# Linear attention with an ELU feature map: v loaded in longer rows, z from one-column products on held weights, five tiles added by GpSimd, one exp for the transposed q

## The chip, the cores and the metric

The kernel runs on one core of a Trainium2 chip. The metric is the device time in microseconds of one execution. The core has five engines that run side by side and meet by semaphores: TensorE (PE in the profile; its weight loads are PEld), VectorE (DVE), ScalarE (ACT), GpSimd (POOL) and SyncE (SP), which here only issues DMA transfers. Sixteen DMA engines serve one queue.

## What is computed

```python
phi_q = jnp.where(q > 0, q + 1, jnp.exp(q)) + 1e-6
phi_k = jnp.where(k > 0, k + 1, jnp.exp(k)) + 1e-6
kv  = jnp.einsum("bhsd,bhse->bhde", phi_k, v)
z   = jnp.einsum("bhsd->bhd", phi_k)
num = jnp.einsum("bhqd,bhde->bhqe", phi_q, kv)
den = jnp.einsum("bhqd,bhd->bhq", phi_q, z)[..., None] + 1e-6
return num / den
```

There are 32 heads of 2048 rows by 128 columns in bf16. q, k and v are 512 KB a head each, and so is the result.

## The kernel before

**A head.** A head is 16 tiles of 128 x 128. The feature map is computed as min(exp(x), 1) + 1e-6 plus max(x, 0); these two parts are kept apart as two arrays (emk and rk for k, emq and rq for q), and their sum is formed by PE, which multiplies both parts and accumulates.

- k: ACT takes exp of all 2048 columns (L263), DVE the min and the added 1e-6 (L269), POOL the relu (L265). For four of the 16 tiles (`ADD`, L164) POOL also adds the two parts (L274), so that PE needs one product for such a tile and not two.
- kv and z (L278 to L293): PE accumulates phi_k^T v in one PSUM bank, `kvz_ps`. The column sum z comes by a column of ones beside v. v lies in SBUF in four groups of four tiles with gaps of ones between them (L166, L223), so the first and the last tile of each group take a neighbouring one as a 129th column. A tile inside a group has none beside it, and a second product of one column with the same weights follows (L288). It loads its weights anew. ACT copies kv to SBUF (L294), DVE adds the two parts of z (L296).
- q: PE transposes 16 tiles to `xT_ps` in two halves (L304, two banks). ACT takes exp of each half (L315) and the relu of the second (L318), DVE the relu of the first (L321) and the min (L324).
- result: PE multiplies each q tile's two parts by kv and z (L333, L334), 129 columns a tile, three tiles to each of five PSUM banks, the 16th tile cut over the first two banks. DVE adds 1e-6 to the denominators (L352), takes reciprocals (L356) and multiplies (L364, L369). For the last two heads this is done in two groups of banks, with one bank on ACT (L378).

**Order.** The order on each engine is written by hand: every operation has a key, mostly the head's number plus a constant, and each engine runs its operations by rising key (`Plan.order`). `place` (L239) holds exceptions for the first and last heads. Waits follow from what each operation reads and writes; a PSUM bank read by two engines is read by one after the other.

**Transfers.** SP issues all loads and stores by the same keys (L255, L394). k, v and q have six buffers each, the result ten. k and q go 128 rows of 4096 bytes a head; v goes 512 rows of 1024 bytes, because of its gaps. Stores are put later and later (key h + 1 + 0.18 h, L398), so that at first nearly only loads are issued and at the end only stores are left.

**Ahead of the first head** POOL makes the identity and the ones (L216 to L223), and PE runs 36 products on the identity (L230).

Of the kernel before, what the change touches and what calls it, by code (L numbers as in the profile page):

```python
# [5 lines left out]
ALU = mybir.AluOpType  # L6
# [138 lines left out]
def bass_standalone__linear_attn_elu__prompt_kernel(  # L145
# [15 lines left out]
    NB = 5  # L161
    HALF = NT * P // 2

    ADD = (1, 2, 5, 6)  # L164
    SPLIT = tuple(j for j in range(NT) if j not in ADD)
    GAP, GRP = 32, 4 * D  # L166
    VW = 4 * GRP + 5 * GAP
# [6 lines left out]
    with ExitStack() as es:  # L174
# [39 lines left out]
        ofull = o_ps[:, :]  # L214

        pl.add("pool", -9, lambda g: g.memset(ident[:], 0.0), writes=[("id0",)])  # L216
# [3 lines left out]
        pl.add("pool", -7, lambda g: g.memset(ones_sb[:], 1.0), writes=[("ones",)])  # L220

        vfull = v_sb[:, :, :]
        pl.add("pool", -7, lambda g: g.memset(_ap(vfull, 0, [[VW, NBI], [GAP + GRP, 5], [1, GAP]]), 1.0), writes=[("vones",)])  # L223

        def warm(n):

            def f(pe):
                for w in range(n):
                    b = 2 + w % 3
                    last = pe.matmul(o_ps[:, b * 512 + 3 * NC: b * 512 + 3 * NC + 125], lhsT=ident[:, :], rhs=ident[:, 0:125],  # L230
                                     start=True, stop=True)
                return last
            return f

        pl.add("pe", -9, warm(36), reads=[("ident",)], writes=[("banko", 2), ("banko", 3), ("banko", 4)])

        place = {("emk", 0): -2.05, ("rq", 0): -2.0, ("emq", 0): -1.9, ("zs", 0): -1.75,  # L239
                 ("emk", 1): -1.8, ("rq", 1): -1.7, ("emq", 1): -1.6, ("emk", 2): -1.4, ("rq", 2): 0.945,  # L240
                 ("ek", 1): -0.97, ("ek", 2): 0.03,
                 ("kv", NH - 1): NH - 2 + 0.75, ("kvs", NH - 1): NH - 2 + 0.05, ("zs", NH - 1): NH - 2 + 0.942}

        for h in range(NH):
# [5 lines left out]
            def load(name, buf, src, key, h=h, bi=bi):  # L250
                dst, rws = buf[:, bi], rows(src, h)
                if name == "v":
                    dst = _ap(vfull, bi * VW + GAP, [[GAP + GRP, 4], [1, GRP]])
                    rws = rws.rearrange("p (a b) -> p a b", b=GRP)
                pl.add("sp", key, lambda sp: sp.dma_start(dst, rws), writes=[(name, bi)], dma=(name, bi))  # L255
# [4 lines left out]

# [11 lines left out]
            def added(x, b3=b3):  # L272
                return _ap(x[:, b3, D:2 * D], 0, [[4 * D, 2], [1, 2 * D]])
# [4 lines left out]
            def kv(pe, tiles, srcs, bi=bi, b3=b3):  # L278
                for j in tiles:
                    for src in srcs:  # L280
                        first, fin = (j == SPLIT[0] and src is emk_sb), j == ADD[-1]
                        w = src[:, b3, j * D:(j + 1) * D]
                        c = GAP + (GAP + GRP) * (j // 4) + D * (j % 4)
                        l, r = (1, 0) if j % 4 == 0 else (0, 1) if j % 4 == 3 else (0, 0)
                        last = pe.matmul(kvz_ps[:, 1 - l:NC + r], lhsT=w, rhs=v_sb[:, bi, c - l:c + D + r], start=first, stop=fin,  # L285
                                         skip_group_check=True)
                        if not l + r:
                            last = pe.matmul(kvz_ps[:, 0:1], lhsT=w, rhs=ones_sb[:, 0:1], start=False, stop=fin,  # L288
                                             skip_group_check=True)
                return last  # L290
            pl.add("pe", at("kv", -1.2), lambda pe, kv=kv: kv(pe, SPLIT, (emk_sb, rk_sb)),
                   reads=[("emk", b3), ("rk", b3), ("v", bi), ("ones",), ("vones",)], writes=[("bankkv",)])
# [6 lines left out]

# [8 lines left out]
            def cols(half):  # L308
                return slice(half * HALF, half * HALF + HALF)

            for half in (0, 1):
                pl.add("pe", h - 1.25 + 0.01 * half, tr(half), reads=[("q", bi), ("ident",)], writes=[("bankx", half)])
            for half in (0, 1):
                pl.add("act", h - 1.1 + 0.05 * half,
                       lambda a, b2=b2, c=cols(half): a.activation(eq_sb[:, b2, c], xT_ps[:, c], ACT.Exp),  # L315
                       reads=[("bankx", half)], writes=[("eq", b2, half)])
            pl.add("act", h - 1.0,
                   lambda a, b3=b3, c=cols(1): a.activation(rq_sb[:, b3, c], xT_ps[:, c], ACT.Relu),  # L318
                   reads=[("bankx", 1)], writes=[("rq", b3, 1)])
            pl.add("dve", at("rq", -2 + 0.948),  # L320
                   lambda d, b3=b3, c=cols(0): d.tensor_scalar(rq_sb[:, b3, c], xT_ps[:, c], 0.0, None, op0=ALU.max),  # L321
                   reads=[("bankx", 0)], writes=[("rq", b3, 0)])
            pl.add("dve", at("emq", -2 + 0.955),
                   lambda d, b2=b2, b3=b3: d.tensor_scalar(emq_sb[:, b3, :], eq_sb[:, b2, :], 1.0, EPS, op0=ALU.min, op1=ALU.add),  # L324
                   reads=[("eq", b2, 0), ("eq", b2, 1)], writes=[("emq", b3)])


            phi = [("emq", b3), ("rq", b3, 0), ("rq", b3, 1), ("kvs", b3), ("zs", b3)]

            def num(bank, b3=b3):  # L330
                def tile(pe, t, col, c0, c1):
                    o_ap = o_ps[:, bank * 512 + col: bank * 512 + col + c1 - c0]
# [4 lines left out]
                def f(pe):  # L337
                    for s in range(3):
                        last = tile(pe, bank * 3 + s, s * NC, 0, NC)
                    if bank < 2:  # L340
                        last = tile(pe, NT - 1, 3 * NC, 64 * bank, 64 * bank + 65)
                    return last
                return f
            for bank in range(NB):
                pl.add("pe", h + 0.7 + 0.001 * bank, num(bank), reads=phi, writes=[("banko", bank)])


            tail = h >= NH - 2
            for g, (b0, b1) in enumerate(((0, 2), (2, NB)) if tail else ((0, NB),)):
                key = h + 0.9 + 0.03 * g  # L350
                banks = [("banko", b) for b in range(b0, b1)]
                pl.add("dve", key, lambda d, b3=b3, b0=b0, b1=b1: d.tensor_scalar(  # L352
                    den_sb[:, b3, 4 * b0:4 * b1].rearrange("p (a b) -> p a b", b=4),
                    _ap(ofull, 512 * b0, [[512, b1 - b0], [NC, 4]]), EPS, None, op0=ALU.add),
                    reads=banks, writes=[("den", b3, g)])
                pl.add("dve", key + 0.01, lambda d, b3=b3, b0=b0, b1=b1: d.reciprocal(  # L356
                    rden_sb[:, b3, 4 * b0:4 * b1], den_sb[:, b3, 4 * b0:4 * b1]),
                    reads=[("den", b3, g)], writes=[("rden", b3, g)])
# [4 lines left out]
            def last_tile(d, bo=bo, rd=rd):  # L363
                return d.tensor_tensor(  # L364
                    out=o_sb[:, bo, NT - 1, :].rearrange("p (a b) -> p a b", b=64),
                    in0=_ap(ofull, 3 * NC + 1, [[512, 2], [1, 64]]), in1=rd(3, [[0, 2], [0, 64]]), op=ALU.mult)

            def div(b0, b1, bo=bo, rd=rd):
                return lambda d: d.tensor_tensor(  # L369
                    out=o_sb[:, bo, 3 * b0:3 * b1, :].rearrange("p (a b) d -> p a b d", b=3),  # L370
                    in0=_ap(ofull, 512 * b0 + 1, [[512, b1 - b0], [NC, 3], [1, D]]),
                    in1=rd(4 * b0, [[4, b1 - b0], [1, 3], [0, D]]), op=ALU.mult)

            def div_act(bank, bo=bo, rd=rd):
                def f(a):
                    for s in range(3):
                        c = 512 * bank + NC * s + 1
                        last = a.activation(o_sb[:, bo, 3 * bank + s, :], o_ps[:, c:c + D], ACT.Copy,  # L378
                                            scale=rd(4 * bank + s, [[1, 1]]))
                    return last  # L380
                return f

            lo, hi = ("rden", b3, 0), ("rden", b3, 1 if tail else 0)
            pl.add("dve", h + 0.92, last_tile, reads=[("banko", 0), ("banko", 1), lo], writes=[("o", bo, "t")])
            pl.add("dve", h + 0.925, div(0, 2), reads=[("banko", 0), ("banko", 1), lo], writes=[("o", bo, 0)])
            if tail:
                pl.add("dve", h + 0.945, div(2, 4), reads=[("banko", 2), ("banko", 3), hi], writes=[("o", bo, 1)])
                pl.add("act", h + 0.95, div_act(4), reads=[("banko", 4), hi], writes=[("o", bo, 2)])
            else:
                pl.add("dve", h + 0.945, div(2, NB), reads=[("banko", b) for b in (2, 3, 4)] + [hi],  # L390
                       writes=[("o", bo, 1), ("o", bo, 2)])
# [7 lines left out]
            if h < NH - 1:  # L399
                store(0, NT, late, ("t", 0, 1, 2), bo)  # L400
            else:
                store(0, 6, late, (0,), bo)
                store(6, 12, late + 0.01, (1,), NBO)
                store(12, 16, late + 0.02, ("t", 2), NBO + 1)
# [30 lines left out]
```

## Time and profile before

| | us |
|---|---|
| time, median of 3 runs | 174.4 (174.22 to 174.61) |
| span of the profiled execution | 172.1 |
| what lies around the span (median less span) | 2.3 |
| median time of a 512 KB load from issue to landing | 11.6 to 11.8 |

The span runs from the first to the last instruction of the profiled execution. The page of the profile gives busy time by engine, the span in 40 slices of 4.3 us each, the DMA queue's packets and bytes, the chain of work that ended last, and groups of equal instructions. The mean granted TensorE clock was 0.990 of full speed. A matmul's duration in these tables (some 220 ns) is its way through a pipeline; what counts for the rate is the distance from one start to the next.

| group | count | mean ns |
|---|---|---|
| L263 ACT exp of k, 128x2048 | 32 | 2160 |
| L315 ACT exp of half of transposed q, 128x1024 | 64 | 1267 |
| L274 POOL addition, 128x512 | 32 | 1153 |
| L265 POOL relu of k, 128x2048 | 32 | 1893 |
| L288 PE one-column products, own weight load | 384 | 166 to 167 |

### The profile page before, as it was taken

The page shows a single profiled execution, that of the slowest core. Times are in us where ns is not written, and L with a number is a line of the kernel's source. Part 1 is how long each engine was busy: PE and PEld are TensorE (multiplying, and loading weights), DVE is VectorE, ACT ScalarE, POOL GpSimd, SP SyncE. Part 2 cuts the span into 40 slices and gives each one's busy share as a digit, 9 for nine tenths or more (in the row PEclk, how much of TensorE's full clock was granted, in tenths as well). Part 3 has the DMA queues.
Part 4 walks back from the last instruction along what each step waited for, and adds up shares of the span by engine and source line. Part 5 has one row for each costly group of instructions (what it writes and reads, how often), then busy time and mean ns, then how long its engine had stood idle before and what let it go on. Part 6 is the DMA issues. An engine that isn't in the chain of part 4 may idle for free.

```text
span 172.1 us, 6707 instructions
## 1 busy us (share of the span) xinstructions
PE 155.7 (90%) x2916; PEld 151.8 (88%) x2916; DVE 149.5 (87%) x292; ACT 155.5 (90%) x167; POOL 98.1 (57%) x72
## 2 busy tenths in 40 slices
PE   6679999999999999999999998999989999997740
PEld 6568999999999999999999898989979988997740
DVE  0345899999999999999999989899998999899880
ACT  3999999999999999999999999999999998996320
POOL 4666667766666666667776654556666456763000
PEclk9999999999999999999999999999999999999995
DMA  5999999999999999999999999999999999999985
GB/s 206 334 411 395 405 398 398 401 407 400 411 396 403 412 408 407 407 403 408 403 406 410 406 406 410 403 406 407 410 408 405 417 396 406 408 407 412 417 348 192
DMA packets 31037, 67.54 MB, mean 392 GB/s; under 512 B 2080, under 2 KB 18848, under 8 KB 31008
## 3 DMA queue, kind: packets, MB, share of 16 engines
q1 hardware_dynamic: 31008, 67.12, 100.4%
q8 instruction: 23, 0.38, 0.8%
q14 instruction: 6, 0.05, 0.1%
HBM read 50.33 MB, written 16.78 MB: 390 GB/s over the span
## 4 chain that ended last, share of the span: by engine, by line
PE 68%; DVE 17%; DMA 7%; SPq 3%; issue 2%; ACT 0%; DVEq 0%
PE kvz_ps L285 29%; PE o_ps L333 14%; PE o_ps L334 13%; PE xT_ps L304 12%; DVE o_sb L369 8%; DMA v_sb<-in_v_dram 7%; SPq L255 3%; DVE rq_sb L321 2%; DVE emq_sb L324 2%; DVE emk_sb L269 2%; DVE o_sb L364 1%; DVE rden_sb L356 1%; DVE den_sb L352 1%; PE kvz_ps L288 1%; DVE kvs_sb L296 0%
## 5 line engine op out<-in xcount | busy, mean ns | idle before, releaser
L315 ACT ACTIVATE eq_sb<-xT_ps 128x1024 bf16<-128x1024 bf16 x64 | 69.7, 1267 | 3.3 <-PE xT_ps L304 2.7
L263 ACT ACTIVATE ek_sb<-k_sb 128x2048 bf16<-128x2048 bf16 x32 | 69.1, 2160 | 2.4 <-DMA k_sb<-in_k_dram 2.3
L369 DVE TENSOR_TENSOR o_sb<-o_ps,rden_sb 128x768 bf16<-128x768 f32 x64 | 70.1, 1135 | 0.0
L274 POOL TENSOR_TENSOR rk_sb<-rk_sb,emk_sb 128x512 bf16<-128x512 bf16 x32 | 36.9, 1153 | 55.6 <-DVE den_sb L352 30.4
L333 PE MATMUL o_ps<-kvs_sb,emq_sb 128*128 128x129 bf16 (+1 forms) x544 | 62.0, 217 | 1.9 <-DVE o_sb L369 1.2
L285 PE MATMUL kvz_ps<-v_sb,rk_sb 128*128 128x129 bf16 (+1 forms) x512 | 63.5, 218 | 0.0
L265 POOL TENSOR_SCALAR rk_sb<-k_sb 128x2048 bf16<-128x2048 bf16 x32 | 60.6, 1893 | 3.7 <-DMA k_sb<-in_k_dram 2.8
L334 PE MATMUL o_ps<-kvs_sb,rq_sb 128*128 128x129 bf16 (+1 forms) x544 | 62.0, 217 | 0.0
L285 PE MATMUL kvz_ps<-v_sb,emk_sb 128*128 128x129 bf16 (+1 forms) x384 | 53.9, 220 | 4.1 <-DMA v_sb<-in_v_dram 1.3
L333 PEld LDWEIGHTS o_ps<-kvs_sb,emq_sb 128*128 128x128 bf16 x544 | 51.4, 98 | 2.4 <-DVE o_sb L369 1.5
L334 PEld LDWEIGHTS o_ps<-kvs_sb,rq_sb 128*128 128x128 bf16 x544 | 50.9, 97 | 0.0
L285 PEld LDWEIGHTS kvz_ps<-v_sb,rk_sb 128*128 128x128 bf16 x512 | 47.5, 97 | 0.0
L285 PEld LDWEIGHTS kvz_ps<-v_sb,emk_sb 128*128 128x128 bf16 x384 | 36.6, 97 | 6.1 <-DMA v_sb<-in_v_dram 2.4
L318 ACT ACTIVATE rq_sb<-xT_ps 128x1024 bf16<-128x1024 bf16 x32 | 41.1, 1284 | 0.0
L304 PE MATMUL xT_ps<-ident,q_sb 128*128 128x128 bf16 x512 | 33.8, 219 | 2.4 <-DMA q_sb<-in_q_dram 1.4
L288 PE MATMUL kvz_ps<-ones_sb,rk_sb 128*128 128x1 bf16 x256 | 34.3, 166 | 0.0
L304 PEld LDWEIGHTS xT_ps<-ident,q_sb 128*128 128x128 bf16 x512 | 29.7, 98 | 3.4 <-DMA q_sb<-in_q_dram 1.8
L269 DVE TENSOR_SCALAR emk_sb<-ek_sb 128x2048 bf16<-128x2048 bf16 x32 | 21.8, 682 | 10.1 <-ACT ek_sb L263 10.1
L288 PEld LDWEIGHTS kvz_ps<-ones_sb,rk_sb 128*128 128x128 bf16 x256 | 23.2, 96 | 0.0
L321 DVE TENSOR_SCALAR rq_sb<-xT_ps 128x1024 bf16<-128x1024 bf16 x32 | 21.8, 680 | 0.9 <-ACT eq_sb L315 0.9
L324 DVE TENSOR_SCALAR emq_sb<-eq_sb 128x2048 bf16<-128x2048 bf16 x32 | 21.9, 684 | 0.5 <-ACT eq_sb L315 0.5
L288 PE MATMUL kvz_ps<-ones_sb,emk_sb 128*128 128x1 bf16 x128 | 21.2, 167 | 0.1
(18 smaller groups left out, 72.8 us busy)
## 6 DMA issues: line engine op xcount, KB each, us to landing
k_sb<-in_k_dram SPq DMA_DIRECT2D x32, 512.0 KB, 11.6
q_sb<-in_q_dram SPq DMA_DIRECT2D x32, 512.0 KB, 11.6
v_sb<-in_v_dram SPq DMA_DIRECT2D x32, 512.0 KB, 11.8
out_dram<-o_sb SPq DMA_DIRECT2D x31, 512.0 KB, 12.2
out_dram<-o_sb SPq DMA_DIRECT2D x2, 192.0 KB, 4.2
out_dram<-o_sb SPq DMA_DIRECT2D x1, 128.0 KB, 3.8
```

The costliest lines, as they stand in the source:

```text
L263: lambda a, bi=bi, b2=b2: a.activation(ek_sb[:, b2, :], k_sb[:, bi, :], ACT.Exp),
L265: pl.add("pool", h, lambda g, bi=bi, b3=b3: g.tensor_scalar(rk_sb[:, b3, :], k_sb[:, bi, :], BIG, 0.0, op0=ALU.min, op1=ALU.max), reads=[( ...
L274: pl.add("pool", h + 0.5, lambda g, added=added: g.tensor_tensor(out=added(rk_sb), in0=added(rk_sb), in1=added(emk_sb), op=ALU.add), reads ...
L285: last = pe.matmul(kvz_ps[:, 1 - l:NC + r], lhsT=w, rhs=v_sb[:, bi, c - l:c + D + r], start=first, stop=fin, skip_group_check=True)
L288: last = pe.matmul(kvz_ps[:, 0:1], lhsT=w, rhs=ones_sb[:, 0:1], start=False, stop=fin, skip_group_check=True)
L304: last = pe.transpose(xT_ps[:, j * P:(j + 1) * P], q_sb[:, bi, j * P:(j + 1) * P], ident[:])
L315: lambda a, b2=b2, c=cols(half): a.activation(eq_sb[:, b2, c], xT_ps[:, c], ACT.Exp),
L318: lambda a, b3=b3, c=cols(1): a.activation(rq_sb[:, b3, c], xT_ps[:, c], ACT.Relu),
L324: lambda d, b2=b2, b3=b3: d.tensor_scalar(emq_sb[:, b3, :], eq_sb[:, b2, :], 1.0, EPS, op0=ALU.min, op1=ALU.add),
L333: pe.matmul(o_ap, lhsT=emq_sb[:, b3, t * P:(t + 1) * P], rhs=kvs_sb[:, b3, c0:c1], start=True, stop=False)
L334: return pe.matmul(o_ap, lhsT=rq_sb[:, b3, t * P:(t + 1) * P], rhs=kvs_sb[:, b3, c0:c1], start=False, stop=True)
L369: return lambda d: d.tensor_tensor(out=o_sb[:, bo, 3 * b0:3 * b1, :].rearrange("p (a b) d -> p a b d", b=3), in0=_ap(ofull, 512 * b0 + 1, ...
```

## The change

- v: rows of 4096 bytes in buffers 0 to 3 (`GROUPS` 1: ones only before and after all 16 tiles), two groups of eight tiles with rows of 2048 bytes in buffers 4 and 5. Every inner tile needs the one-column product for z: 23 products a head in buffers 0 to 3 and 19 in 4 and 5, for 12 before.
- That product is issued as a matmul instruction with no weight load; it uses what the product before it has loaded (`mm_held`).
- POOL adds the two parts for tiles 1 to 5 (`ADD`), which lie side by side.
- One ACT exp covers all 2048 columns of the transposed q.
- The products ahead of the first head are 42, on a zeroed piece of the result buffer that DVE writes.
- First heads: for head 0, DVE takes the relu of all of q; its result products come before kv of head 1, and several places change. Last heads: kv of head 31 comes before the result products of head 30; head 31's first two result groups go to the banks of `xT_ps`; denominators, reciprocals and products are cut finer, with two groups on ACT for each of the last two heads.

```diff
-    ADD = (1, 2, 5, 6)
+    LAST = NH - 1
+    ADD = (1, 2, 3, 4, 5)
-    GAP, GRP = 32, 4 * D
-    VW = 4 * GRP + 5 * GAP
+    GAP = 32
+    GROUPS = (1, 1, 1, 1, 2, 2)
+    VW = NT * D + 3 * GAP
+        def vcol(bi, j):
+            n = NT // GROUPS[bi]
+            return GAP * (j // n + 1) + D * j, j % n == 0, j % n == n - 1
+        def mm_held(pe, out_ap, rhs, stop):
+            return pe.add_instruction(mybir.InstMatmult(
+                start_tensor_calc=False, stop_tensor_calc=stop, ldweights=False, bass_skip_group_check=True,
+                tile_position=(0, 0), tile_size=(P, P), name=nc.get_next_instruction_name(), engine=mybir.EngineType.PE,
+                ins=[pe.lower_ap(rhs), pe.lower_ap(held[0])], outs=[pe.lower_ap(out_ap)]))
-        pl.add("pe", -9, warm(36), reads=[("ident",)], writes=[("banko", 2), ("banko", 3), ("banko", 4)])
+        pl.add("pe", -9, warm, reads=[("warm",)], writes=[("banko", 2), ("banko", 3), ("banko", 4)])
-        place = {("emk", 0): -2.05, ("rq", 0): -2.0, ("emq", 0): -1.9, ("zs", 0): -1.75,
-                 ("emk", 1): -1.8, ("rq", 1): -1.7, ("emq", 1): -1.6, ("emk", 2): -1.4, ("rq", 2): 0.945,
-                 ("ek", 1): -0.97, ("ek", 2): 0.03,
-                 ("kv", NH - 1): NH - 2 + 0.75, ("kvs", NH - 1): NH - 2 + 0.05, ("zs", NH - 1): NH - 2 + 0.942}
+        place = {("ek", 1): -1.05, ("ek", 2): -0.05, ("ek", 3): 0.95,
+                 ("emk", 0): -2.05, ("rq", 0): -2.0, ("emq", 0): -1.9, ("zs", 0): -1.75,
+                 ("emk", 1): -1.7, ("rq", 1): -1.6, ("emq", 1): -1.5, ("emk", 2): 0.93, ("zs", 1): 0.946,
+                 ("num", 0): -0.22,
+                 ("zs", LAST): LAST - 1 + 0.9, ("kvs", LAST): LAST - 1 + 0.72}
-                    dst = _ap(vfull, bi * VW + GAP, [[GAP + GRP, 4], [1, GRP]])
-                    rws = rws.rearrange("p (a b) -> p a b", b=GRP)
+                    n = GROUPS[bi]
+                    dst = _ap(vfull, bi * VW + GAP, [[GAP + NT * D // n, n], [1, NT * D // n]])
+                    rws = rws.rearrange("p (a b) -> p a b", a=n)
-                return _ap(x[:, b3, D:2 * D], 0, [[4 * D, 2], [1, 2 * D]])
+                return x[:, b3, ADD[0] * D:(ADD[-1] + 1) * D]
                         if not l + r:
-                            last = pe.matmul(kvz_ps[:, 0:1], lhsT=w, rhs=ones_sb[:, 0:1], start=False, stop=fin,
-                                             skip_group_check=True)
+                            held[0] = w
+                            last = mm_held(pe, kvz_ps[:, 0:1], ones_sb[:, 0:1], fin)
-            for half in (0, 1):
-                pl.add("act", h - 1.1 + 0.05 * half,
-                       lambda a, b2=b2, c=cols(half): a.activation(eq_sb[:, b2, c], xT_ps[:, c], ACT.Exp),
-                       reads=[("bankx", half)], writes=[("eq", b2, half)])
+            both = [("bankx", 0), ("bankx", 1)]
+            pl.add("act", h - 1.1, lambda a, b2=b2: a.activation(eq_sb[:, b2, :], xT_ps[:, :], ACT.Exp),
+                   reads=both, writes=[("eq", b2)])
+            cut = NT * P if h == 0 else HALF
+            def where(g, h=h):
+                if h < LAST:
+                    return ofull, 512 * g, ("banko", g)
+                return (xfull, 512 * g, ("bankx", g)) if g < 2 else (ofull, 512 * (0, 1, 4)[g - 2], ("banko", (0, 1, 4)[g - 2]))
+            else:
+                den(0, 2, h + 0.9)
+                rec(0, 2, h + 0.905)
+                div_act(1, h + 0.91)
+                div(0, 1, h + 0.91)
+                last_tile(h + 0.915)
+                den(2, 4, h + 0.92)
+                den(4, 5, h + 0.922)
+                rec(2, 5, h + 0.925)
+                div_act(4, h + 0.93)
+                div(2, 4, h + 0.93)
```

## The prediction

> **What bounds the kernel now.** I read the engine sums and the transfer queue first, then who waited for whom, then the chain in its steady part, then single starts.
>
> ```profile
> PE 155.7 (90%) x2916; PEld 151.8 (88%) x2916; DVE 149.5 (87%) x292; ACT 155.5 (90%) x167; POOL 98.1 (57%) x72
> ...
> DMA  5999999999999999999999999999999999999985
> GB/s 206 334 411 395 405 398 398 401 407 400 411 396 403 412 408 407 407 403 408 403 406 410 406 406 410 403 406 407 410 408 405 417 396 406 408 407 412 417 348 192
> ...
> q1 hardware_dynamic: 31008, 67.12, 100.4%
> ```
>
> Four engines lie between 87% and 90%, and the DMA engines are full from the second of 40 slices to the 38th; only the last two slices sag. So two things can set the end: the queue's bytes, or an engine that is a little dearer per head than the others. The waits from 20 to 74 us tell which it is early on:
>
> ```profile
> POOL rk_sb L274 <- DVE den_sb L352: 18.7, 11, 2.3
> POOL rk_sb L274 <- DVE emq_sb L324: 1.6, 1, 1.6
> DVE den_sb L352 <- PE o_ps L334: 0.5, 1, 0.5
> ```
>
> That is the whole answer: nobody waits for a load, and PE never waits. The chain from 20 to 60 us is PE alone:
>
> ```profile
> 21.55 0.89 PE xT_ps L304 x16
> ...
> 26.17 0.89 PE xT_ps L304 x16
> ...
> 30.78 0.89 PE xT_ps L304 x16
> ...
> 40.02 0.89 PE xT_ps L304 x16
> ```
>
> One head costs PE (40.02 - 21.55) / 4 = 4.617 us. ACT needs 4.67 (its big exp starts at 57.69, 62.36, 67.03) and DVE 4.65 (its two division products start at 59.56, 64.21, 68.86). From 100 us the big exp starts at 105.54, 115.56, 125.40, 135.62, 145.79: 5.03 us a head. The k loads for these heads were issued at 93.96, 102.28, 113.66, 124.63 and 133.07; the median of 11.6 us to landing makes 105.6, 113.9, 125.3, 136.2, 144.7. So the second half is paced by the queue: three loads and a store per head take it longer than PE takes. At the end both meet: DVE ends at 167.5, and the stores run out behind it. To gain, the change must shorten the queue and must not lengthen an engine beyond what the queue gives back.
>
> **v in longer rows (the queue).** Two windows with different mixes give the price of a packet; 20 to 60 us is 16 x 40 = 640 us of engine time, with 4426 packets of 1 KB and 2802 of 4 KB:
>
> ```profile
> DMA packets 7725, 16.13 MB, mean 403 GB/s; under 512 B 489, under 2 KB 4915, under 8 KB 7717
> q1 hardware_dynamic: 7717, 16.01, 103.4%
> ```
>
> 152 to 164 us is 192 us of engine time, with 332 and 1118:
>
> ```profile
> DMA packets 1601, 4.94 MB, mean 412 GB/s; under 512 B 149, under 2 KB 481, under 8 KB 1599
> q1 hardware_dynamic: 1599, 4.92, 102.3%
> ```
>
> As both are full, two equations give 44.2 ns for 1 KB and 158.6 ns for 4 KB. Taking the share column instead (103.4% and 102.3%, packets overlapping) gives 47.1 and 161.7. A row of v costs four of the first now and one of the second afterwards: 18.2 ns less, or 26.9. Two packets of 2 KB, between the two by a straight line, save 12.1 or 17.9. Buffers 0 to 3 serve 22 heads, buffers 4 and 5 ten; each engine moves 8 rows a head: 22 x 8 x 18.2 + 10 x 8 x 12.1 = 4.2 us, or 6.2. I take 5. The queue's own end then moves from about 171.8 (0.3 us of slack in the sagging slices) to 166.8. SP issues the same transfers in the same order, so no queue is passed.
>
> The Trainium skill, "DMA: Bandwidth & Descriptors", section "Why small descriptors are slow (HBM only)", prices a packet at one cycle per 32 bytes and about 3 more, so a row saves 4 x 35 - 131 = 9 cycles, or 6 as two packets: at the 850 MHz of the same page that is, as an estimate, 2.4 us in all. The windows say about twice that; by the rule the queue would end at 169.4 and the time would be 171.7.
>
> **z on held weights (PE).** Each inner tile's one-column product now loads its weights again. Starts from 103 us:
>
> ```profile
> 103.05 0.22 PE L285 MATMUL kvz_ps<-v_sb,emk_sb 128*128 128x128 bf16 x1
> 103.10 0.17 PE L288 MATMUL kvz_ps<-ones_sb,emk_sb 128*128 128x1 bf16 x1
> ...
> 103.38 0.22 PE L285 MATMUL kvz_ps<-v_sb,emk_sb 128*128 128x129 bf16 x1
> ```
>
> Four pairs take 0.33 us, so 82.5 ns a pair; 16 transposes take 0.89 us, 56 ns each; the one-column product costs 26.5 ns. Longer rows leave fewer seams with ones beside them, so more tiles need it: 23 a head in buffers 0 to 3, 19 in 4 and 5, mean 21.6, against 12. A product without a load is nowhere in this trace. Below, its own column alone: 129 columns start 57 ns apart, 65 columns 29, so a column is 0.44 ns and one column some 3 ns. Above, a full slot of 56 ns, if the next load can't start beside it. I take 26, the same product's row less next to nothing, because the next tile's load still has to run. The fifth added tile saves one product of 56.5. A head: 4.617 - 12 x 0.0265 - 0.0565 + 21.6 x 0.026 = 4.805 us. This is an addition of 0.19 us a head: **PE becomes the dearest engine.**
>
> **POOL, ACT, DVE.** GpSimd's addition grows from 1.153 us to 1.153 x 640 / 512 = 1.44. It starts at 63.65 and would end at 65.09; PE starts that head's products at 63.86 and comes to the added tiles after 22 x 0.0565 + 18 x 0.026 = 1.71 us, at 65.57: hidden, by 0.5 us (without that cover it would cost 0.3 us a head). One exp for two: 128x1024 takes ACT 0.90 us from start to next start, 128x128 takes 0.16, so 0.054 is fixed and 4.67 becomes 4.61; off the path, as PE is dearer. Its wait for the second eight transposes is 0.45 us longer; behind it stand the relu, the kv copy and the next exp, all of which PE needs half a head later. DVE's middle heads are unchanged at 4.65.
>
> **First and last heads.** Before, the products of head 2 start at 17.64, when its v lands. Three v loads come 0.5 us sooner in all, but head 0's division now stands ahead of the one-column sum of head 1 that these products wait for; DVE has 0.6 us more (relu of the whole q) and ACT 0.9 less. Sooner by the loads alone would be 17.1; DVE's list of heads 0 and 1, laid end to end behind the first exp (8.4), brings that sum to 17.9. I leave 17.64. At the end, kv of head 31 goes before the result products of head 30 and the last head uses the two transpose banks too; the waits of 0.7 us that PE has at 159 and 163 go.
>
> **The sum.** PE: 17.64 + 29 x 4.805 = 157.0 for the start of kv 31; its own 27 x 0.0565 + 23 x 0.026 = 2.1; two heads of result products, 30 x 0.057 + 4 x 0.03 = 1.83 each, 3.7; the division after the last of them 1.9 (now PE's last product starts at 165.4 and DVE ends at 167.5; the finer cut saves 0.2); 0.4 to issue the last store; 2.4 to land (the shortest k load takes 3.3 from issue to landing, and 128 KB in place of 512 saves 0.9 at 412 GB/s); 0.5 to the end of the span, as now. That is 168.0, later than the queue's 166.8, so PE sets the end. The span before is 172.1 and the median of the runs 174.4, 2.3 above it: **170.3 us**.
>
> **Rivals.**
> - *A held product is nearly free* (anything up to some 20 ns). For it: nothing but the load fills its 26.5 ns. Against: nothing in the trace shows it. Then the queue sets the end: 166.8 + 2.3 = 169.1. The Trainium skill, "TensorE: Matmul & The Clock Gate", section "Wait — 56ns, not 53.3ns?", says starts never come closer than about 25 ns however narrow the product; no run here shows it for held weights, and by it this rival falls and the sum is 169.6.
> - *Held products cost more than a load hides.* The place is the gap between the held product and the next tile's load, if that load no longer runs ahead past two products. Each ns adds 21.6 x 29 + 23 = 0.65 us to the path; 168.0 becomes 172.1 at 26 + 4.1 / 0.65 = 32 ns, and beyond it the kernel is slower. At a full slot of 56 ns it is 168.0 + 30 x 0.65 + 2.3 = 189.8. Against: 27 ns is enough for a load now.
> - *The queue gives half*: the fixed part of a packet overlaps more than two windows can tell. Then 2.1 us, the queue ends at 169.7, the time is 172.0; with nothing saved, 174.1. The Trainium skill's price of a packet, above, points here.
> - *A new wait in the first or last heads* (the later one-column sum, or the exp that waits for both halves) adds 1 to 2 us: 171.3 to 172.3.
>
> **Chances.** Forecast 0.50, held nearly free 0.25, held dear 0.12, queue gives half or nothing 0.08, new wait 0.05. The measurement of this kernel can tell 0.2% (0.35 us) from no change. Faster: 0.50 + 0.25 + 0.05 + 0.03 = 0.83; slower 0.12 + 0.01 = 0.13; same 0.04. The range runs from the queue at its larger saving (172.1 - 0.3 - 6.2 + 2.3 = 167.9) up to a held product of about 30 ns (172.8), which leaves out the dear end and the queue that saves nothing.
>
> **What would show it.** Right: PE starts a transpose group every 4.8 us in mid-kernel with no PE wait; the q1 share of engine time about 5 us lower; 5,376 v packets for 16,384; DVE and ACT waiting a little for PE. The one-column line's start to the next start reads the held price directly. Wrong: that gap above 32 ns or near 3; the added tiles waiting for POOL; mid-kernel GB/s still at 405; PE waiting for DVE or ACT after 100 us as now.

## The result, and the profile of the changed kernel

The changed kernel takes 171.97 us (171.81 to 172.86) beside 174.47 for the kernel before in the same comparison: a ratio of 0.9866, 95% interval [0.9838, 0.9894]. The span of its profiled execution is 170.0 us, 2.0 below the median. The forecast of 170.3 had the direction and the bound; the time lies 1.7 us above it, inside the range.

From the page of the changed kernel: the engine sums, the moved bytes in 40 slices, the queue, and the shares of the chain that ended last.

```profile
PE 158.6 (93%) x3202; PEld 156.1 (92%) x2506; DVE 153.2 (90%) x295; ACT 156.1 (92%) x140; POOL 105.5 (62%) x72
...
GB/s 204 363 417 418 419 407 417 415 411 422 407 418 412 414 421 412 416 416 410 416 414 413 424 412 412 415 412 422 414 416 418 414 416 412 414 422 409 359 266 174
...
q1 hardware_dynamic: 20000, 67.12, 98.1%
...
PE 81%; DMA 7%; DVE 5%; SPq 3%; issue 1%; ACT 1%
```

The queue moves the same 67.12 MB in 20,000 packets for 31,008; the difference, 11,008, is 16,384 - 5,376, the packets of v. Mid-kernel it goes at about 415 GB/s for 405, and it sags over three slices at the end where it sagged over two: it has slack now. PE is 81% of the chain. Its weight loads (PEld) are 696 fewer than its products, 2506 for 3202: the one-column products do load nothing. What a head costs is read from the chain in its steady part (start, length, work):

```profile
99.49 0.89 PE xT_ps L315 x16
104.32 0.89 PE xT_ps L315 x16
109.16 0.89 PE xT_ps L315 x16
113.98 0.89 PE xT_ps L315 x16
```

These are heads with whole rows of v, 4.83 us each; heads with two packets a row take 4.74. From the first such group at 22.83 to the last at 152.22 it is 129.39 / 27 = 4.79 us a head, and from 20 to 160 us PE has no wait. So in its second half too the kernel is paced by PE, no longer by loads.

The rest of the difference lies at the two ends. The start, in the chain and on DVE (start, length, operation, in brackets the idle time before it):

```profile
5.68 11.70 DMA v_sb<-in_v_dram
17.38 1.34 issue
18.73 0.33 PE kvz_ps L297 x3
```

```profile
8.27 1.23 DVE L326 TENSOR_SCALAR rq_sb<-xT_ps 128x2048 bf16<-128x2048 bf16 x1 [1.58 <-ACT eq_sb L322]
9.41 2.06 DVE L333 TENSOR_SCALAR emq_sb<-eq_sb 128x2048 bf16<-128x2048 bf16 x1
...
13.34 0.69 DVE L326 TENSOR_SCALAR rq_sb<-xT_ps 128x1024 bf16<-128x1024 bf16 x1 [1.13 <-PE o_ps L349]
...
15.27 0.95 DVE L388 TENSOR_TENSOR o_sb<-o_ps,rden_sb 128x768 bf16<-128x768 f32 x1
16.14 1.09 DVE L282 TENSOR_SCALAR emk_sb<-ek_sb 128x2048 bf16<-128x2048 bf16 x1
17.15 1.34 DVE L388 TENSOR_TENSOR o_sb<-o_ps,rden_sb 128x1152 bf16<-128x1152 f32 x1
18.41 0.21 DVE L308 TENSOR_SCALAR kvs_sb<-kvz_ps 128x1 bf16<-128x1 f32 x1
```

v of head 2 is there at 17.38, but its products start at 18.73. The chain calls the 1.34 us between "issue"; the list of DVE shows what it is: the one-column sum of head 1 (L308), which empties the PSUM bank, runs at 18.41, behind head 0's division (L388 twice) and the min of head 2 (L282). The end, on DVE:

```profile
162.51 0.29 DVE L381 TENSOR_TENSOR o_sb<-o_ps,rden_sb 128x128 bf16<-128x128 f32 x1 [0.36 <-ACT o_sb L399]
...
165.39 0.29 DVE L381 TENSOR_TENSOR o_sb<-xT_ps,rden_sb 128x128 bf16<-128x128 f32 x1 [0.36 <-ACT o_sb L399]
```

DVE has work without a break from 157 to 167 us except for these two waits, where the 16th tile's product stands behind ACT's read of the bank that both share. PE waits 0.18 us at 162.86 and 0.48 at 164.20 for DVE, and the last product of DVE ends 2.6 us after PE's last product starts.

### The profile page after: what moved, and what is told of

The parts are those of the page before. It is cut to its first block, busy times and chain, and to the rows that moved or that the text cites. A ratio compares the mean times of both kernels' runs of the same rounds, so it can differ in the third digit from the quotient of the medians.

```text
span 170.0 us, 6563 instructions
## 1 busy us (share of the span) xinstructions
PE 158.6 (93%) x3202; PEld 156.1 (92%) x2506; DVE 153.2 (90%) x295; ACT 156.1 (92%) x140; POOL 105.5 (62%) x72
## 3 DMA queue, kind: packets, MB, share of 16 engines
q1 hardware_dynamic: 20000, 67.12, 98.1%
## 4 chain that ended last, share of the span: by engine, by line
PE 81%; DMA 7%; DVE 5%; SPq 3%; issue 1%; ACT 1%
PE kvz_ps L297 34%; PE o_ps L348 16%; PE o_ps L349 16%; PE xT_ps L315 15%; DMA v_sb<-in_v_dram 7%; SPq L269 3%; DVE o_sb L388 2%; PE kvz_ps L236 1%; ACT o_sb L399 1%; DVE rden_sb L376 1%; DVE o_sb L381 1%; DVE rq_sb L326 0%; DVE emq_sb L333 0%; DVE den_sb L370 0%; DVE kvs_sb L308 0%
## 5 line engine op out<-in xcount | busy, mean ns | idle before, releaser
L287 POOL TENSOR_TENSOR rk_sb<-rk_sb,emk_sb 128x640 bf16<-128x640 bf16 x32 | 44.7, 1396 | 48.2 <-DVE emq_sb L333 45.4
L297 PE MATMUL kvz_ps<-v_sb,rk_sb 128*128 128x128 bf16 (+1 forms) x512 | 69.1, 217 | 0.0
L388 DVE TENSOR_TENSOR o_sb<-o_ps,rden_sb 128x768 bf16<-128x768 f32 (+2 forms) x63 | 68.9, 1132 | 0.1
L322 ACT ACTIVATE eq_sb<-xT_ps 128x2048 bf16<-128x2048 bf16 x32 | 60.1, 1877 | 4.9 <-PE xT_ps L315 3.7
L236 PE MATMUL kvz_ps<-ones_sb,rk_sb 128*128 128x1 bf16 x428 | 59.6, 165 | 0.0
L297 PE MATMUL kvz_ps<-v_sb,emk_sb 128*128 128x128 bf16 (+1 forms) x352 | 56.8, 218 | 2.9 <-issue 1.5
L236 PE MATMUL kvz_ps<-ones_sb,emk_sb 128*128 128x1 bf16 x268 | 44.0, 165 | 0.0
L330 ACT ACTIVATE rq_sb<-xT_ps 128x1024 bf16<-128x1024 bf16 x31 | 31.6, 1018 | 0.0
L282 DVE TENSOR_SCALAR emk_sb<-ek_sb 128x2048 bf16<-128x2048 bf16 x32 | 22.3, 696 | 6.1 <-ACT ek_sb L276 6.1
L326 DVE TENSOR_SCALAR rq_sb<-xT_ps 128x1024 bf16<-128x1024 bf16 (+1 forms) x32 | 22.7, 709 | 3.3 <-ACT eq_sb L322 2.2
L381 DVE TENSOR_TENSOR o_sb<-o_ps,rden_sb 128x128 bf16<-128x128 f32 x31 | 9.0, 291 | 1.4 <-ACT o_sb L399 0.4
```

What stands on the lines that cost most here:

```text
L236: return pe.add_instruction(mybir.InstMatmult(start_tensor_calc=False, stop_tensor_calc=stop, ldweights=False, bass_skip_group_check=True, ...
L287: pl.add("pool", h + 0.5, lambda g, added=added: g.tensor_tensor(out=added(rk_sb), in0=added(rk_sb), in1=added(emk_sb), op=ALU.add), reads ...
L322: pl.add("act", h - 1.1, lambda a, b2=b2: a.activation(eq_sb[:, b2, :], xT_ps[:, :], ACT.Exp), reads=both, writes=[("eq", b2)])
L330: lambda a, b3=b3: a.activation(rq_sb[:, b3, HALF:], xT_ps[:, HALF:], ACT.Relu),
L388: pl.add("dve", key, lambda d: d.tensor_tensor(out=o_sb[:, bo, 3 * g0:3 * g1, :].rearrange("p (a b) d -> p a b d", b=3), in0=_ap(full, bas ...
```

## The experiments

My theory: whole rows of v shorten the queue, and this is the gain; PE is now the bound at 4.79 us a head, and what the time lost against the forecast lies in the first and last heads. Rivals: that the held weights matter, that the single exp is the late start, that the queue still sets the end. The kernel before had medians of 174.03 to 174.47 in these comparisons, so differences of up to 0.4 us between runs of different ones say little by themselves; each ratio is to the kernel before in its own. Gains over the changed kernel are given below as differences of medians; by the ratios they come out up to 0.2 us different.

### Held weights or own load

Each one-column product loads its weights again:

```diff
-                            held[0] = w
-                            last = mm_held(pe, kvz_ps[:, 0:1], ones_sb[:, 0:1], fin)
+                            last = pe.matmul(kvz_ps[:, 0:1], lhsT=w, rhs=ones_sb[:, 0:1], start=False, stop=fin,
+                                             skip_group_check=True)
```

> The changed kernel, with each one-column product loading its weights again. Theory (PE paces the middle, and a held product costs as much as one that loads, 27 ns to the next start in both): the transpose groups keep their distance of 4.79 us and the time stays at 172.0 us, within 0.3. Rival (a held product saves PE something that single starts do not show, or takes load off the rest): 2 ns for each of 696 products is 1.4 us, so 173.4 or more.

Measured: 172.24 us (171.69 to 173.59), ratio 0.9905 [0.9876, 0.9934], an interval that overlaps the changed kernel's. PE's starts, first of the changed kernel, then of this one:

```profile
105.33 0.22 PE L297 MATMUL kvz_ps<-v_sb,emk_sb 128*128 128x128 bf16 x1
105.38 0.17 PE L236 MATMUL kvz_ps<-ones_sb,emk_sb 128*128 128x1 bf16 x1
...
105.66 0.22 PE L297 MATMUL kvz_ps<-v_sb,emk_sb 128*128 128x128 bf16 x1
```

```profile
106.94 0.22 PE L297 MATMUL kvz_ps<-v_sb,emk_sb 128*128 128x128 bf16 x1
107.00 0.17 PE L300 MATMUL kvz_ps<-ones_sb,emk_sb 128*128 128x1 bf16 x1
...
107.27 0.22 PE L297 MATMUL kvz_ps<-v_sb,emk_sb 128*128 128x128 bf16 x1
```

Four pairs take 0.33 us in both. The median from the one-column start to the next start is 27 ns in both, and the transposes come every 4.79 us in both. The mm_held part of the change is worth nothing that can be measured.

### The held product in the other order

Why 27 ns? The forecast's reason was the next tile's load. Here the one-column product comes first, with the load, and the 128 columns follow on held weights, so that no load stands behind the short product.

```diff
                         if not l + r:
                             held[0] = w
-                            last = mm_held(pe, kvz_ps[:, 0:1], ones_sb[:, 0:1], fin)
+                            pe.matmul(kvz_ps[:, 0:1], lhsT=w, rhs=ones_sb[:, 0:1], start=False, stop=fin, skip_group_check=True)
+                            last = mm_held(pe, kvz_ps[:, 1:NC], v_sb[:, bi, c:c + D], fin)
```

> The changed kernel, with the order of each pair turned round: the one-column product comes first and loads the weights, the 128-column product holds them. Theory as the prediction put it (the 27 ns behind a one-column product are the next tile's load, which can start only when that product starts): now no load stands behind it, the distance to the next start falls to some 3 ns and the load runs beside the 128 columns; PE's head falls by 21.7 x 0.024 = 0.52 us to 4.27, DVE's 4.65 and the queue take over, 170.6 to 171.0 us as in e3. Rival (two products never start closer than about 27 ns, whatever is loaded): the distance stays at 26 to 27 ns, 172.0 us.

```profile
105.17 0.22 PE L236 MATMUL kvz_ps<-v_sb,rk_sb 128*128 128x128 bf16 x1
105.22 0.17 PE L302 MATMUL kvz_ps<-ones_sb,emk_sb 128*128 128x1 bf16 x1
105.25 0.22 PE L236 MATMUL kvz_ps<-v_sb,emk_sb 128*128 128x128 bf16 x1
...
105.49 0.22 PE L236 MATMUL kvz_ps<-v_sb,rk_sb 128*128 128x128 bf16 x1
```

Still 27 ns from the one-column start (105.22) to the next (105.25), now a product that loads nothing, and 4.79 us a head. So the load is not the reason; two starts do not come closer here, whatever is loaded. The Trainium skill, "TensorE: Matmul & The Clock Gate", section "Wait — 56ns, not 53.3ns?", says that starts never come closer than about 25 ns however narrow the product; the traces agree, at 27 ns for held and loaded weights alike. The time is 173.37 us (171.74 to 173.58), 0.992 [0.9888, 0.9952]. Its profiled execution, with a span of 169.9, has the changed kernel's pitch and start. The median lies 1.4 us higher because four of its six executions took 173.3 us or more, and these four show a lower granted clock (last section).

### Rows of 1 KB, the rest of the change kept

```diff
-    GROUPS = (1, 1, 1, 1, 2, 2)
+    GROUPS = (4, 4, 4, 4, 4, 4)
```

> The changed kernel, with v in rows of 1024 bytes in all six buffers as before (13 one-column products a head for 21.75). Theory: PE's price of a head falls to 4.59 us, but the queue paces the second half again (5.03 us a head, mean rate near 405 GB/s for 415): 173.5 to 174.5 us, so that longer rows are the whole of the gain. Rival (the gain comes from the single exp and the new first and last heads, and PE is what is dear): PE has 0.2 us a head less to do, 172.0 falls to 168 or less.

174.18 us (173.62 to 174.56), 1.0007 [0.9993, 1.0021]: all of the gain is gone, though PE has fewer one-column products. The page of this run:

```profile
GB/s 199 314 409 400 404 404 399 400 412 404 401 408 402 411 405 405 411 401 406 406 407 412 403 405 409 401 410 405 409 409 403 412 404 410 402 407 416 415 358 139
...
q1 hardware_dynamic: 31008, 67.12, 100.0%
```

The queue is full to the 38th slice again, at 405 GB/s. Without longer rows there is no gain: everything else in the change, taken together, neither gains nor loses with the old rows. That longer rows alone would bring the gain doesn't follow (see the run with four added tiles), and the kernel before with nothing but longer rows was not run.

### Without the inner one-column products

```diff
-                        if not l + r:
+                        if not l + r and src is None:
```

> The changed kernel without the one-column products: z has only the rows of the first and last tile of each group, so the denominators are too small. Theory (PE is the bound): PE's head falls by 21.7 x 0.027 = 0.59 us to 4.2, ACT and DVE (4.61 and 4.65) and the queue are next, and the end moves only as far as the queue allows: its sagging last slices hold about 1.6 us, so 170.0 to 170.8 us. Rival (the queue sets the end already): 172.0, within 0.3. Rival (the queue is far from the end): 29 heads at DVE's 4.65, 139.2 - 134.9 = 4.3 us less, 167.7.

This kernel leaves out a part of z. 170.95 us, 0.9819 [0.9796, 0.9843]. With 0.6 us a head taken off PE the time falls by 1.0 us only (0.8 by the ratios). The chain and the last stores:

```profile
DVE 77%; DMA 7%; issue 4%; ACT 3%; PE 3%; SPq 2%
...
out_dram<-o_sb SPq DMA_DIRECT2D x2, 192.0 KB, 4.9
out_dram<-o_sb SPq DMA_DIRECT2D x1, 128.0 KB, 4.3
```

PE is out of the chain, and stores of 192 KB take 4.9 us to land for 1.9 in the changed kernel: they stand behind others in the queue. So in this run the queue's own end is at a span of 169.2, not at 166.8 as I had it.

### The start, the tail, and both

Start: the min of head 2 and the one-column sum of head 1 get their places of before, so that the sum comes ahead of head 0's division. Tail: for the last two heads the 16th tile's product goes ahead of ACT's read of its bank.

```diff
-                 ("emk", 1): -1.7, ("rq", 1): -1.6, ("emq", 1): -1.5, ("emk", 2): 0.93, ("zs", 1): 0.946,
+                 ("emk", 1): -1.7, ("rq", 1): -1.6, ("emq", 1): -1.5, ("emk", 2): -1.4,
...
                 rec(0, 2, h + 0.905)
+                last_tile(h + 0.907)
                 div_act(1, h + 0.91)
                 div(0, 1, h + 0.91)
-                last_tile(h + 0.915)
```

> The changed kernel, with two places of the first heads as before: the min of head 2's exp and the one-column sum of head 1 stand ahead of head 0's division on DVE again. Theory (the 1.1 us that the first products of head 2 start later, 18.7 for 17.6, are paid at the end, as PE has no slack after them): these products start at about 17.4 and the time is 170.6 to 171.1 us. Rival (the queue or the tail would take the gain back): they start at 17.4 and the time stays at 172.0.

> The changed kernel; in the last two heads the 16th tile's product on DVE is put ahead of ACT's share of the second bank, which both engines read. Theory (the last 10 us are DVE's, from 157.1 to 167.1, with two waits of 0.36 us for ACT that the new split brought): 0.7 us less, 171.3 us. Rival (the queue's last stores set the end): no change, 172.0. Rival (ACT now waits and is late itself): slower, up to 172.4.

> The places of e4 and the order of e5 together. Theory that PE's path alone sets the end: both gains add, 171.0 - 0.7 = 170.3 us. Theory that the queue's own end was reached in e4 already (e3, with PE out of the way, had 170.95 us and a queue full to the last two slices): 170.8 to 171.0, the gain of the tail is lost behind the stores.

Start alone: 171.02 us, 0.9823 [0.9802, 0.9843]. PE, DVE and POOL of that run:

```profile
14.93 1.89 POOL L278 TENSOR_SCALAR rk_sb<-k_sb 128x2048 bf16<-128x2048 bf16 x1 [1.54 <-DVE emq_sb L333]
```

```profile
15.21 2.17 DVE L282 TENSOR_SCALAR emk_sb<-ek_sb 128x2048 bf16<-128x2048 bf16 x1 [0.43 <-ACT ek_sb L276]
...
17.38 0.21 DVE L308 TENSOR_SCALAR kvs_sb<-kvz_ps 128x1 bf16<-128x1 f32 x1
```

```profile
17.69 0.22 PE L297 MATMUL kvz_ps<-v_sb,emk_sb 128*128 128x129 bf16 x1 [0.93 <-DVE kvs_sb L308]
```

The one-column sum comes at 17.38 for 18.41, and kv of head 2 starts at 17.69 for 18.73: 1.04 us of PE's path, and 0.95 us of the time (0.75 by the ratios, whose intervals just touch). The order of the changed kernel puts that sum at 18.25 to 18.76 in six more runs: own loads, other order, old rows, no inner products, tail, six added tiles. This is the place where the forecast lost its first microsecond.

Tail alone: 171.56 us (170.66 to 172.53), 0.9844 [0.9808, 0.9879]. DVE's two waits of 0.36 are gone; from its product for the last banks of head 30 to its very last product it takes 2.50 us (164.39 to 166.89) for 2.94 (163.18 to 166.12). The median is 0.4 us lower as well, but the interval overlaps the changed kernel's. The median hides two groups: three executions took 170.66 to 170.93 us, about 1 us less than three of the changed kernel's four (171.81 to 172.05); the other three, the profiled one among them, took 172.20 to 172.53 at a lower granted clock (last section).

Both: 170.68 us, 0.9795 [0.9774, 0.9815], 0.3 us better than the start alone, with intervals that overlap. kv of head 2 starts at 17.04, and DVE ends at 165.15 for 167.08, 1.9 us earlier; the time is only 1.3 us less. The page tells where the rest went:

```profile
out_dram<-o_sb SPq DMA_DIRECT2D x2, 192.0 KB, 3.1
out_dram<-o_sb SPq DMA_DIRECT2D x1, 128.0 KB, 2.9
```

The last store, issued at 165.56, lands at 168.41: 2.9 us for 2.0, behind the queue.

### Four added tiles, and six

```diff
-    ADD = (1, 2, 3, 4, 5)
+    ADD = (1, 2, 3, 4)
```

> The changed kernel, with GpSimd adding tiles 1 to 4 and not 5, so that PE has one more product with its one-column product a head, 83 ns. Theory (PE paces every head from the third on): 29 x 0.083 = 2.4 us more, 174.4 us, the distance of transpose groups 4.87 us. Rival (the queue or POOL paces it): within 0.5 us of 172.0.

175.02 us (173.78 to 175.91, without the profiled execution, which took 177.35 at a granted clock of 0.971), 1.003 [1.0008, 1.0053]: 0.3% slower than the kernel before. The transposes come every (157.62 - 26.01) / 27 = 4.87 us, 0.08 more than with five, one product of 56 ns and one of 27, as priced. (The profiled execution starts late too, at 26.01 for 22.83; only its pitch is used.) So longer rows gain nothing with four added tiles, and five added tiles gain nothing with the old rows: it takes both.

With `ADD = (1, 2, 3, 4, 5, 6)`:

> The changed kernel, with GpSimd adding tiles 1 to 6. Theory (PE paces the middle and POOL's cover of 0.5 us is not used up by 0.28 us more): 83 ns less a head on PE, 4.71 us, 29 x 0.083 = 2.4 us less up to what the queue allows, 170.6 to 171.0 us. Rival (POOL becomes the bound: its addition of 1.67 us, its relu of 1.89 and the 1.3 us in which it stands aside for two DVE operations make 4.86 us a head): transposes every 4.86 us or more, 174 us.

171.17 us, 0.981 [0.9787, 0.9833], 0.8 us better than the changed kernel; the profiled execution is the shortest, with 170.15 us and a span of 168.3, 1.7 less than the changed kernel's. Its transposes start at 22.84 and, 27 heads later, at 150.16, every 4.72 us: PE's saving of 0.08 us a head is there nearly in full. But POOL's additions start at 61.01, 65.74 and 70.47, every 4.73, whether PE needs 4.74 or 4.65 us for the head, so a second bound lies right behind PE. Two engines show what sets it, first POOL, then DVE:

```profile
62.62 1.89 POOL L278 TENSOR_SCALAR rk_sb<-k_sb 128x2048 bf16<-128x2048 bf16 x1
65.74 1.64 POOL L287 TENSOR_TENSOR rk_sb<-rk_sb,emk_sb 128x768 bf16<-128x768 bf16 x1 [1.23 <-DVE den_sb L370]
```

```profile
64.30 0.76 DVE L282 TENSOR_SCALAR emk_sb<-ek_sb 128x2048 bf16<-128x2048 bf16 x1
64.98 0.68 DVE L333 TENSOR_SCALAR emq_sb<-eq_sb 128x2048 bf16<-128x2048 bf16 x1
65.58 0.16 DVE L370 TENSOR_SCALAR den_sb<-o_ps 128x20 f32<-128x20 f32 x1
```

POOL's relu ends at 64.51, DVE's min of k (0.76 for 0.68) at 65.06, its min of q at 65.66, and POOL's next addition starts 0.08 later, at 65.74. The kernel makes the addition wait for that min of q (`emq` among its reads). The bracket names the denominators, but those it doesn't wait for: in the changed kernel an addition starts at 66.05, 0.08 after the min ended and before the denominators end (66.12). So the addition, the relu and DVE's two mins close a ring of 4.73 us. DVE is 64% of this run's chain, PE 23%. A seventh tile would lengthen the ring by what it adds to POOL (my reading; not tried, and neither was the addition without its wait for the min).

### The exp in halves

```diff
-            pl.add("act", h - 1.1, lambda a, b2=b2: a.activation(eq_sb[:, b2, :], xT_ps[:, :], ACT.Exp),
-                   reads=both, writes=[("eq", b2)])
+            for half in (0, 1):
+                pl.add("act", h - 1.1 + 0.05 * half,
+                       lambda a, b2=b2, half=half: a.activation(eq_sb[:, b2, half * HALF:(half + 1) * HALF],
+                                                                xT_ps[:, half * HALF:(half + 1) * HALF], ACT.Exp),
+                       reads=both[half:half + 1], writes=[("eq", b2, half)])
```

> The changed kernel, with the exp of transposed q in two halves again. Theory (ACT has slack beside PE's 4.79 us a head): ACT pays 0.05 us more a head, 4.66, PE does not see it, 172.0 us within 0.3. Rival (ACT is next to the bound and the coupling costs): 29 x 0.05 = 1.5 us more, 173.5. Rival (the single exp's wait for all 16 transposes costs in the first heads): the first products of head 2 start sooner and the time falls by up to 0.5.

171.19 us, 0.9815 [0.9797, 0.9833]: 0.8 us better than the changed kernel. DVE's relu of q starts earlier, a little for head 0 and 1.9 us for head 1, and kv of head 2 with it. First the changed kernel's exp for head 1 on ACT, then DVE with halves:

```profile
11.36 1.88 ACT L322 ACTIVATE eq_sb<-xT_ps 128x2048 bf16<-128x2048 bf16 x1 [0.29 <-PE xT_ps L315]
```

```profile
7.96 1.23 DVE L329 TENSOR_SCALAR rq_sb<-xT_ps 128x2048 bf16<-128x2048 bf16 x1 [1.17 <-ACT eq_sb L324]
...
11.40 0.68 DVE L329 TENSOR_SCALAR rq_sb<-xT_ps 128x1024 bf16<-128x1024 bf16 x1
...
17.30 0.21 DVE L308 TENSOR_SCALAR kvs_sb<-kvz_ps 128x1 bf16<-128x1 f32 x1
```

In the changed kernel that relu starts at 13.34, 0.10 after the single exp has ended (11.36 + 1.88 = 13.24), since DVE reads a bank after ACT. With halves it follows the first half. The one-column sum is 1.1 us earlier (17.30 for 18.41) and the pitch is the same 4.79. One exp for two saves nothing in the steady part, where ACT isn't the bound, and costs 0.8 us in the first heads.

### All four, and whole rows everywhere

Start, tail, six added tiles and halves together; then the same with `GROUPS = (1, 1, 1, 1, 1, 1)`.

> Four edits at once: the start and the tail as in the runs on them, the exp of transposed q in halves again, and GpSimd adding six tiles. Theory (the queue's own end is the floor, at a span of about 168.3 to 169.2, where the runs with the start, with six added tiles and without inner one-column products all ended): the transposes come 1 to 1.5 us earlier at the start and every 4.71 us, some 3.5 to 4 us earlier at the end than in the changed kernel, and almost all of that is lost behind the stores: 170.0 to 170.8 us, no better than the best single edit, with the queue full to its last slice but one. Rival (the edits add up, TensorE is still the bound): 0.95 + 0.8 + 0.8 + 0.4 us off 171.97, less what start and halves share: 169.0 to 169.6.

> The same four edits, and v in whole rows in all six buffers. It takes 2 x 128 of the 2 KB packets and puts 128 of 4 KB in their place in ten heads, about 0.07 us of queue each by the packets' durations, 0.7 us in all, and adds four one-column products of 27 ns in each of these heads, 1.1 us of TensorE in all. Theory (queue is the bound once TensorE has 3 us of slack): 0.4 to 0.8 us faster than the run before it, 169.4 to 170.2. Rival (TensorE the bound): 0.5 to 1.1 us slower than the run before it.

170.87 us, 0.9794 [0.9777, 0.9812], and 170.59 us, 0.9777 [0.9761, 0.9793]. The first:

```profile
DVE 73%; issue 10%; PE 8%; ACT 5%
...
out_dram<-o_sb SPq DMA_DIRECT2D x2, 192.0 KB, 4.8
out_dram<-o_sb SPq DMA_DIRECT2D x1, 128.0 KB, 4.6
```

The edits do not add up. DVE ends at 163.4, 3.7 us earlier than in the changed kernel, and the span is only 1.2 us shorter: the last stores take 4.6 to 4.8 us. Whole rows everywhere have the better median by 0.3 us, in the direction of a queue that binds, but the intervals overlap. Both beat the kernel before and the changed one; neither is better than the start and the tail alone (170.68) by more than the measurement tells.

## Why the prediction was right, and where it was off

- **The bound and the direction held.** PE became the dearest engine, the chain is PE, and the queue got slack. The pitch was forecast at 4.805 and is 4.79; 29 heads took 139.0 us for 139.3. The price of a one-column product (26 ns taken, 27 found) was right, its reason wrong: it is not the next tile's load. That the weights are held changes nothing. The rivals "nearly free" and "dear" fall with it. That 171.97 lies inside the range is in part luck: the upper end of 172.8 stood for a held product of 30 ns, which isn't what came.
- **The queue was mis-sized.** I took 5 us off its end. The packets' time fell by about as much as the share column said: 100.4% of 172.1 is 172.8 us, 98.1% of 170.0 is 166.8, 6.0 less (6.2 by that column). But the kernels that run into the queue (no inner products, start and tail, all four) end at spans of 168.8 to 169.2, and the old rows at 172.7; in time 3.2 to 3.5 us, less than the 4.2 by rates. The run with six added tiles ended at 168.3, so the queue's end is no sharper than that. The time in packets is not the time at the end; packets overlap (a share above 100% says so). The price of a packet by the Trainium skill, "DMA: Bandwidth & Descriptors", section "Why small descriptors are slow (HBM only)", gave, as an estimate, 2.4 us and an end at 169.4, which was nearer to these 168.8 to 169.2 than my 166.8 was, though its saving is too small. It did no harm to the sum, as PE ended later still, but it hid that only about 1 us was left to gain behind PE: the 169.1 of the rival "nearly free" could not have come.
- **"I leave 17.64" failed.** The start came at 18.73, 1.1 us later. I had laid DVE's list end to end and got 17.9 for the one-column sum; it was 18.41. The list itself was the better guide, and I left it for the place of before. Yet 17.9 doesn't come out of the list either: by the distances of starts in the changed kernel's trace its operations from the relu of all of q up to the sum take 7.1 us, which behind 8.4 makes 15.5. What the list lacked is the wait for the single exp of head 1. DVE's relu of that head starts at 13.34, and from there DVE works with hardly a break to 18.41, 0.4 us of it in a min that stands behind POOL (last section). The other min behind POOL, 1.4 us longer than alone, falls into this wait: in the run with own loads it took 0.69 and the sum still came at 18.46. The prediction had the exp's longer wait and let it go, because what stands behind it is needed "half a head later"; in the first heads it cost 0.8 us.
- **The tail was mis-sized.** "The waits of 0.7 us that PE has at 159 and 163 go" and a division of 1.9 us: PE has 0.66 us of waits, at 162.86 and 164.20, and DVE ends 2.6 us after PE's last start. Together 1.4 us more. Landing took 2.0 for 2.4.
- The account on the span: 168.0 + 1.1 (start) - 0.3 (heads) + 0.2 (PE's list at the end as it stands) + 0.7 (its waits) + 0.7 (division) - 0.4 (landing) = 170.0. What lies around the span was 2.0 for 2.3, so 171.97.
- The rival "a new wait in the first or last heads", 171.3 to 172.3, is what came, on top of the forecast's mechanism. (The rival "the queue gives half" names 172.0 as well, but the queue gave more than half and didn't set the end.) I gave it 0.05, for want of walking through DVE's list at both ends against what POOL and ACT do at that moment. POOL's addition was hidden as forecast; with six tiles its ring with DVE is as long as PE's head.
- Of the signs named, one hardly showed: DVE and ACT wait for PE only once each between 20 and 160 us.

## What to carry to other kernels

When a change lengthens rows to relieve a full queue, price its end by a rate between two full stretches, not by the time in packets (here even the rate promised more than came), and see how little the next bound leaves: here PE, the queue and the ring of POOL and DVE lie within 2%, so four edits that gave 0.4 to 1 us singly by their medians gave 1.1 us together. A change in the order of the first heads is worth a walk through the whole list of the engine that gets more work there, with the other engines' operations of that moment beside it. An operation merged on an engine that isn't the bound gains nothing in the steady part and can cost in the first and last heads. Before a difference of 1 us is read from medians, see whether the executions had the same granted clock.

## What the runs showed of the hardware

- **DVE's min waits for POOL, whole.** In the changed kernel's start POOL's relu and DVE's min overlap:

```profile
9.04 1.89 POOL L278 TENSOR_SCALAR rk_sb<-k_sb 128x2048 bf16<-128x2048 bf16 x1 [0.80 <-DMA k_sb<-in_k_dram]
...
14.79 1.89 POOL L278 TENSOR_SCALAR rk_sb<-k_sb 128x2048 bf16<-128x2048 bf16 x1 [1.10 <-DVE den_sb L370]
```

The relu ends at 10.93 and 16.68, the mins (2.06 from 9.41, 1.09 from 16.14) at 11.47 and 17.23, 0.54 and 0.55 after it; in the run on the start the relu ends at 16.82 and the min, 2.17 long, at 17.38. Alone a min takes 0.68. It ends as if it did all its work after POOL had ended. The Trainium skill, "SBUF — State Buffer", section "Who interferes with whom", says that the two engines share one port pair as an exclusive lock, which operations of the min's kind can need and those with one SBUF input and no such mode do not. The rows agree on both: the division at 15.27, from PSUM, took 0.95 beside the same relu, and 0.96 alone at the end.
- **Two starts on PE 27 ns apart** (26 at the least) are the closest seen here, for one column, with and without a weight load.
- **A granted clock at one half for 3.41 us.** The tenths of the clock by slice, in the run with own loads, then two stretches of that run (us; busy time and number of instructions of PE, PEld, DVE, ACT and POOL; granted clock, DMA share, GB/s):

```profile
PEclk9999879999999999999999999999999999999998
```

```profile
20.16:23.57 3.41, 3.41 (x45) 3.41 (x42) 1.30 (x2) 3.41 (x4) 1.78 (x2) 0.50 1.03 408
23.57:27.00 3.43, 3.43 (x75) 3.43 (x73) 2.53 (x6) 1.80 (x2) 1.92 (x2) 1.00 1.05 419
```

Slices 5 and 6 have 0.8 and 0.7 because the clock is at one half from 20.16 to 23.57 us: PE gets through 45 products there, in the next stretch through 75. The chain's first group of transposes is at 24.40 for 22.83, and the span is 171.6 for 170.0 at the same pitch. The runs with old rows and with the tail alone have one such stretch of 3.41 us too, that with four tiles two; the changed kernel's profile has none. Half of 3.41 us is 1.7 us of PE's work, and 0.010 of the mean clock over 170 us. The executions fall apart by about that: with own loads 171.7 to 172.3 us at mean clocks of 0.993 to 0.997, and 173.3 to 173.6 at 0.986 and 0.987; with the tail alone 170.7 to 170.9 at 0.993 to 0.997, and 172.2 to 172.5 at 0.987 to 0.989; in the other order likewise, and with six added tiles by about 1 us. The kernel before, which its queue paces, doesn't fall apart so (174.40 us at 0.996 and 174.23 at 0.980 in one comparison). So the scatter fits this stretch in place and size, though only the profiled executions show it directly. Before each of these stretches PE was busy for no more than 1.5 to 1.8 of 3.41 us, in its waits of the first heads; in the run with six tiles it was busy for 1.75 us from 15.12 on and none followed, so what brings it about is open.
